# Attention and token mixing on one core: values in column tiles, keys in halves of 32, shared triangles, another order of the engines' work

## The chip, the cores and the metric

The kernel runs on one core of a Trainium2 chip. The metric is device time in microseconds of one launch, from inputs in HBM to the output in HBM. The engines that matter are TensorE (PE), ScalarE (ACT), VectorE (DVE), GpSimd (POOL) and SyncE (SP), which issues the transfers. Each runs its own instructions in the order of its program and waits on semaphores of the others.

## The reference

Sequence 2048, width 512, 32 heads of 16, a causal window of 256 keys, and a token-mixing MLP of 1792, all with two modulated layer norms:

```python
mod = (_silu(c) @ w_mod).reshape(c.shape[0], 6, 1, -1)
h = _layernorm(x) * (1 + ca) + sa
qkv = (h @ wqkv).reshape(B, S, 3, H, Dh).transpose(2, 0, 3, 1, 4)
scores = einsum('bhqd,bhkd->bhqk', q, k) * Dh ** (-0.5)
mask = (i - j >= 0) & (i - j < 256)          # i: query, j: key
p = softmax(where(mask, scores, -1e9))
o = einsum('bhqk,bhkd->bhqd', p, v) -> (B, S, D) @ wo
x = x + ga * o
h = _layernorm(x) * (1 + cb) + sb
h = _layernorm(h)
u = gelu(einsum('bsd,sf->bdf', h, w1) + b1)
y = einsum('bdf,fs->bds', u, w2) + b2        # then transposed back
x = x + gb * y
```

## The kernel before

**Groups and units.** The tokens are taken in four groups G of 512. `proj(G)` normalises the group's tokens (`xn`), transposes them by DMA into `h1T` and projects queries, keys and values. The attention works in units: 256 queries (a half group, `H`) and eight heads (`g8`, one of four). That is 32 units. PE handles a unit in four tiles of 32 rows, two heads of 16 in each, so that four matmuls run side by side, one per tile `j`.

**Keys, values and sums.** `KT` holds, for each block of 64 keys, 128 columns: the 64 keys with the rows of one head of the two (the other's rows zeroed with `mask_par`), then the same with the rows of the other. So the 128 output partitions of a score matmul are two heads times 64 keys, and its columns are queries. `VT` has the same order of rows, with 32 columns for the two heads, and zeros where the head doesn't match. `ones_bd` has it too, and gives the sums of the softmax. The value and sum matmuls are column tiles: four of 32 columns run side by side.

To make `VT`, group 0 projects values with the two parities in two column tiles of 64. From group 1 on, `v` (L972) computes 128 tokens in the natural order, so that half of each tile has to change partitions: `e_vx` swaps it by two DMAs on SP (`vs<-vb`), and `e_vp` places the own and the swapped half with `tensor_copy`, on POOL or DVE. `VT[1]` is zeroed by POOL and `VT[2]` by two DMAs for it.

**Chunks.** The scores of a unit cover eight blocks of 64 keys, of which the first and last per query block are triangles, computed whole and then masked. They are cut into chunks of 512 columns: NEAR, FAR, and half of MID, which two units share (`pair`, L438). A pair of units thus has five chunks. There are 14 pairs; the four units of the first half group have five chunks of their own. That gives 75 chunks, and chunk numbers below count from 0.

For each chunk `attention` (L1161) issues: scores (`S`, into `pss`, three banks, and `psb`, one), two exponentials on ACT (`EA` of 1536 elements and `EB` of 512, into `et`), a masking multiplication on DVE (`M`). When a unit's chunks are through, the values and sums (`AV`, into `po`), then a logarithm and an exponential on ACT (`lz`, the inverse of the sum), and a product on DVE (`OT`).

**Around it.** `post(G)` multiplies with `wo` (`pa`), adds to x, and runs two layer norms (`h`, `hb`) on POOL and DVE. `partials` accumulates the first MLP matmul (`pu`) over the `hb` that exist, between the chunks; `tail` does the rest after the last chunk (`pu`), the gelu, and the last matmul (`py`).

**The order.** All work up to `py` is a list of 1165 operations (`op`). `ORDER` (L62) is a list of their numbers, and `run_schedule` (L164) emits them in it. `CHOSEN` (L118) names the engine for those that have a choice. So each engine's program order is written out by hand. A run of PE work between two `AV` is split into column tiles, too, when it is short (`NEAR_RUN`, `Op.quad`, `mm` at L415), since the array then keeps its shape.

Every instruction is recorded through a helper, so most of the profile has one line number, L256, and groups are told apart by their tiles.

Of the kernel before, what the change touches and what calls it, by code (L numbers as in the profile page):

```python
# [10 lines left out]
ALU = mybir.AluOpType  # L11
# [5 lines left out]
H = 32  # L17
# [6 lines left out]
KB = 64  # L24
HQ = 4 * KB
# [190 lines left out]
def kernel(  # L216
# [31 lines left out]
    class Ordered:  # L248
        def __init__(self, engine):
            self.engine = engine  # L250
# [1184 lines left out]
```

## Time and profile before

| | |
|---|---|
| median of 3 runs | 254.74 us (253.11, 255.09, 254.74) |
| span of the profiled execution | 252.3 us |
| median above that span | 2.4 us |
| granted TensorE clock | 1.000 over the span |
| start of chunk 0's first exponential | 11.2 us |
| start of chunk 70's first exponential | 162.0 us |
| matmuls | 3949 |

The profile is of one execution, and its own time is not listed apart from its span; what lies around the span is taken as the difference to the median. Times inside it count from its start. A busy share says how long an engine had something in flight. For PE that includes the tail of each pipelined matmul, so that short ones side by side look longer than the columns that they stream. ACT and DVE also overlap an instruction's end with the next one's start; the pace is read from starts.

### The profile page before, as it was taken

To read this page: it belongs to the slowest core of one execution; us is meant where nothing else is said; L and a number is where in the kernel's file an instruction comes from. 1 tells how busy PE (TensorE), PEld (TensorE's weight loads), DVE (VectorE), ACT (ScalarE), POOL (GpSimd) and SP (SyncE) were. 2 spreads that over 40 slices of the span, in tenths; PEclk is the share of its full clock that TensorE was granted. 3 is DMA by queue.
4 is the path that set the end of the run, shared out by engine and by line. 5 is a ranking of instruction groups with operands and counts; after the bars stand their busy time and mean duration, and the time that the engine had idled before them with its cause. 6 is when DMAs were issued, how large, how long until landed. Compare 5 with 4: busy or idle time off the path is not lost.

```text
span 252.3 us, 9189 instructions
## 1 busy us (share of the span) xinstructions
PE 235.3 (93%) x3949; PEld 126.0 (50%) x3949; DVE 205.4 (81%) x408; ACT 179.5 (71%) x254; POOL 126.3 (50%) x228
## 2 busy tenths in 40 slices
PE   7988888899987889999999999999999999999995
PEld 2656644445554544555546454556444444444443
DVE  5499998989989998999897999999978764444443
ACT  4699998999999999999999999997147510000000
POOL 8268968795899989845886348173000000000000
PEclk9999999999999999999999999999999999999999
DMA  6999364356055200003401536314999201111111
GB/s 200 323 351 294 48 47 86 44 70 187 3 74 112 53 23 3 4 3 104 131 3 45 155 82 189 105 44 113 343 388 386 108 22 43 44 52 52 42 44 42
DMA packets 42625, 28.13 MB, mean 111 GB/s; under 512 B 12376, under 2 KB 38488, under 8 KB 42584
## 3 DMA queue, kind: packets, MB, share of 16 engines
q1 hardware_dynamic: 42576, 27.54, 39.4%
q8 instruction: 31, 0.51, 0.9%
q14 instruction: 10, 0.08, 0.1%
q10 hardware_dynamic: 8, 0.00, 0.0%
HBM read 22.03 MB, written 2.10 MB: 96 GB/s over the span
## 4 chain that ended last, share of the span: by engine, by line
PE 52%; ACT 24%; DVE 7%; DMA 5%; issue 5%; POOL 4%; SPq 1%; POOLq 0%; DVEq 0%
ACT et L256 20%; PE py L256 19%; PE pu L256 16%; PE po L256 5%; PE pss L256 5%; ACT lz L256 3%; PE pa L256 3%; DMA x<-in_A_x_dram 2%; DVE et L256 2%; DMA h1T<-xn 2%; DMA wmod<-in_w_mod_dram 1%; POOL h1T L256 1%; PE pq L256 1%; DVE st L256 1%; PE pk L256 1%
## 5 line engine op out<-in xcount | busy, mean ns | idle before, releaser
L256 ACT ACTIVATE et<-pss 128x1536 bf16<-128x1536 f32 x75 | 110.7, 1476 | 2.8 <-PE psb L256 2.3
L256 PE MATMUL py<-guT,w2r 128*128 128x512 bf16 (+2 forms) x238 | 48.7, 366 | 0.0
L256 ACT ACTIVATE et<-psb 128x512 bf16<-128x512 f32 x75 | 46.9, 626 | 0.0
L256 DVE TENSOR_TENSOR et<-et,maskt 128x1024 bf16<-128x1024 bf16 (+2 forms) x79 | 46.4, 603 | 0.1
L256 PE MATMUL pu<-hb,w1s 128*32 128x512 bf16 (+1 forms) x302 | 39.0, 380 | 0.2 <-DVE QT L256 0.2
L256 PEld LDWEIGHTS <-w2r 128*128 128x128 bf16 x238 | 22.8, 98 | 26.1 <-issue 0.3
L256 PE MATMUL pss<-QT,KT 32*128 32x64 bf16 (+3 forms) x720 | 29.9, 230 | 6.2 <-ACT et L256 3.5
L256 PE MATMUL po<-et,VT 128*32 128x64 bf16 (+3 forms) x960 | 32.2, 234 | 1.3 <-DVE kb L256 0.6
L256 PE MATMUL po<-et,ones_bd 128*32 128x256 bf16 (+3 forms) x624 | 31.7, 268 | 0.0
L256 PEld LDWEIGHTS <-KT 32*128 32x128 bf16 x960 | 17.1, 92 | 28.5 <-issue 24.6
L256 DVE TENSOR_TENSOR otile<-py,xr 128x512 bf16<-128x512 f32 (+2 forms) x17 | 11.2, 660 | 24.4 <-PE py L256 24.2
L256 POOL TENSOR_SCALAR KT<-kb,mask_par 128x512 bf16<-128x512 bf16 (+1 forms) x36 | 25.0, 707 | 11.4 <-DVE kb L256 11.1
L256 PE MATMUL psb<-QT,KT 32*128 32x64 bf16 (+3 forms) x240 | 29.3, 231 | 0.0
L256 PEld LDWEIGHTS <-VT 128*32 128x32 bf16 x960 | 20.8, 96 | 13.2 <-issue 4.7
L256 PE MATMUL pk<-h1T,wqkv 128*32 128x512 bf16 (+4 forms) x228 | 21.1, 340 | 2.4 <-DVE OT L256 1.0
L256 DVE BATCH_NORM_STATS2 st<-x 128x6 f32<-128x512 bf16 x32 | 21.5, 680 | 2.1 <-DMA x<-in_A_x_dram 2.1
L256 PEld LDWEIGHTS <-wqkv 128*32 128x32 bf16 (+1 forms) x350 | 15.3, 96 | 12.7 <-issue 4.7
L256 PEld LDWEIGHTS <-w1s 128*32 128x32 bf16 (+1 forms) x302 | 14.1, 97 | 15.0 <-issue 1.5
L256 PE MATMUL pv<-wqkv,h1T 128*32 128x512 bf16 (+2 forms) x202 | 17.1, 348 | 1.3 <-DVE OT L256 0.7
L256 PE MATMUL pu<-hb,w1r 128*128 128x512 bf16 (+1 forms) x96 | 17.9, 380 | 0.0
L256 PE MATMUL pa<-wod,OT 128*32 128x512 bf16 (+1 forms) x136 | 17.2, 381 | 0.0
L256 PEld LDWEIGHTS <-ones_bd 128*32 128x32 bf16 x624 | 15.8, 97 | 0.1
(109 smaller groups left out, 350.1 us busy)
## 6 DMA issues: line engine op xcount, KB each, us to landing
w2r<-in_B_w_dram SPq DMA_DIRECT2D x14, 512.0 KB, 10.2
w1s<-in_B_w_dram SPq DMA_DIRECT2D x19, 256.0 KB, 4.0
w1r<-in_B_w_dram SPq DMA_DIRECT2D x9, 256.0 KB, 4.3
x<-in_A_x_dram SPq DMA_DIRECT2D x16, 128.0 KB, 5.2
wmod<-in_w_mod_dram SPq DMA_DIRECT2D x4, 512.0 KB, 7.8
out_dram<-otile SPq DMA_DIRECT2D x15, 128.0 KB, 1.7
wmod<-in_w_mod_dram SPq DMA_DIRECT2D x4, 256.0 KB, 3.9
wqkv<-in_A_wqkv_dram SPq DMA_DIRECT2D x4, 256.0 KB, 5.7
```

The lines of the kernel that those rows point to most:

```text
L256: ins = call(*args, **kwargs)
```

## The change

1. **Keys in halves of 32.** A block's 128 columns in `KT` become (half, parity, 32 keys) where they were (parity, 64 keys). `ones_bd`, `mask_half` and the masks follow. `emit_masks` builds ten masks of 32 columns, with 6 selections and 16 copies on POOL (4 and 6 before).
2. **Values in column tiles.** `values` projects 32 tokens of one parity per matmul, in four column tiles, so that the result stands in the rows where `VT` needs it, in all groups. The swap by DMA, its copies and the zeroing of `VT[1]` and `VT[2]` are gone; `place` multiplies with `mask_half` and writes zeros with the values. `v` counts as `AV` for the rule on short runs.
3. **Shared triangles.** In the first four of the 14 pairs (two of group 0, two of group 1), NEAR and FAR take the parts of the triangles' blocks that are not empty, and the 32 x 32 triangles that remain go into a middle chunk of 256 columns: a lower triangle in the rows of the first half of the keys, an upper one in those of the second. The exponentials of that chunk have 768 and 256 elements. Two masks then write two copies of it, each with the other half's rows zero, and the values take both.
4. **Another order.** `ORDER` and `CHOSEN` are new throughout, and each instruction depends, without a semaphore, on the one before it on its engine.

```diff
-NEAR = [(-1, 0, 4, 0), (0, 0, 4, 256)]
-FAR = [(-2, 0, 3, 0), (3, 3, 1, 192), (-4, 0, 1, 256), (1, 1, 3, 320)]
-MID = [(-3, 0, 2, 0), (2, 2, 2, 128)]
+MIXED = 4
+NEAR = [(-1, 0, 8, 0), (0, 0, 8, 256)]
+FAR = [(-2, 0, 6, 0), (3, 6, 2, 192), (-4, 0, 2, 256), (1, 2, 6, 320)]
+MID = [(-3, 0, 4, 0), (2, 4, 4, 128)]
+NEAR_MIXED = [(-1, 0, 7, 0), (3, 7, 1, 224), (-4, 0, 1, 256), (0, 1, 7, 288)]
+FAR_MIXED = [(-2, 0, 5, 0), (2, 5, 3, 160), (-3, 0, 3, 256), (1, 3, 5, 352)]
...
                 if pinned[0]:
                     tc.keep_in_program_order(ins)
+                    if self.last is not None:
+                        tc.add_manual_dep(ins.ins, self.last, ...)
+                    self.last = ins.ins.name
...
+    def values(dst, h1T, tb, n):
+        wv = wqkv[:, :, 2 * D : 3 * D].rearrange("p j (a two d) -> p j two a d", two=2, d=DH)
+        for dc in range(ND):
+            for r in range(4):
+                tok = tb * P + n * KB + r // 2 * QB
+                te.matmul(
+                    dst[QB * r : QB * (r + 1), n, :].rearrange("p (a d) -> p a d", d=DH),
+                    lhsT=h1T[:, dc, tok : tok + QB], rhs=wv[:, dc, r % 2, :, :],
+                    start=(dc == 0), stop=(dc == ND - 1), tile_position=(0, QB * r), skip_group_check=True,
+                )
+
+    def place(eng, dst, src, tb, half):
+        eng.tensor_scalar(
+            out=dst[:, 2 * tb : 2 * tb + 2, :, half * DH : (half + 1) * DH],
+            in0=src[:].rearrange("p i (a d) -> p i a d", d=DH),
+            scalar1=mask_half[:, half : half + 1], scalar2=0.0, op0=ALU.mult, op1=ALU.add,
+        )
...
-            vx = op("vx", "SP", 1.05, e_vx, deps=[ve_op], pos=pos, extra=0.1)
-            own = op("vo", {"POOL": 0.78, "DVE": 0.45}, 0.78, lambda e: e_vp(e, True), deps=[ve_op] + war + zeros[r3], pos=pos)
-            b = op("vp", {"POOL": 0.78, "DVE": 0.45}, 0.78, lambda e: e_vp(e, False), deps=[vx] + war + zeros[r3], pos=pos)
+            vx = op("vx", "SP", 0.0, lambda e: None, deps=[ve_op], pos=pos, extra=-2.0)
+            placed = [
+                op(("vo", "vp")[half], {"POOL": 0.78, "DVE": 0.45}, 0.78,
+                   lambda e, half=half: place(ENGINE[e], VT[r3], box["vb", tb], tb, half), deps=[ve_op] + war, pos=pos)
+                for half in range(2)
+            ]
...
+                for unit, kb, qs, nq, col in pieces:
+                    if kb is not None:
+                        score(unit, kb, QB * qs, QB * nq, col)
+                    else:
+                        for qb in range(4):
+                            for side in range(2):
+                                score(unit, qb - 4 * side, KB * qb + QB * side, QB, col + QB * qb, side)
...
+                if masks is None:
+                    halves = et_of[i][:].rearrange("p j (h n s) -> p h j n s", h=2, s=KB)
+                    src = halves[:, 0]
+                    for m0, dst in ((UPPER, halves[:, 1]), (LOWER, src)):
+                        msk = m[:, m0 : m0 + KB].unsqueeze(1).unsqueeze(1).to_broadcast([P, 4, 4, KB])
+                        ve.tensor_tensor(out=dst, in0=src, in1=msk, op=ALU.mult)
+                    return
...
+                if kb is None:
+                    for side in range(2):
+                        for qb in range(4):
+                            value(0, qb - 4 * side, KB * qb + QB * side, QB, col + 256 * side + QB * qb)
```

In `score`, a `side` picks one half of the 128 columns of `KT`, so the tile has 32 rows and 64 columns, and the two halves go to the lower and the upper 64 partitions of the same bank.

Laid side by side, the two built programs differ like this in what each engine does (instructions):

| engine | before | after |
|---|---|---|
| PE | 3949 matmuls, the array's shape changes 160 times | 4807 matmuls, 640 of 32 columns; 158 changes |
| ACT | 75 large exponentials | 71 large and 4 of 768 elements; two copies of keys, one of queries and one of values more |
| DVE | 12 + 12 multiplications of h; 2 splits of keys; 4 copies into VT | 7 + 7; 8; 6 placements into VT |
| POOL | 44 copies into VT, 8 placements, 4 + 4 multiplications of h | none, 26, 9 + 9 |
| SP | 24 swaps, 2 zeroings | none |

More of the change, by code (lines that the diff above doesn't have):

```diff
@@ L24 @@
 KB = 64
+QB = 32
 HQ = 4 * KB
@@ L175, in run_schedule @@
     for run in runs:
-        sums = [n for n, o in enumerate(run) if o.name == "AV"]
+        sums = [n for n, o in enumerate(run) if o.name == "AV" or o.name == "v"]
         if run[0].cls == "AV" and sums:
@@ L250, in __init__ @@
             self.engine = engine
+            self.last = None
         def __getattr__(self, name):
@@ L300 @@
     wod = const.tile([P, ND, D], BF, name="wod")
-    maskt = const.tile([P, 3, KB], BF, name="maskt")
+    maskt = const.tile([P, 10, QB], BF, name="maskt")
     ones_bd = const.tile([P, 2 * DH], BF, name="ones_bd")
     nc.gpsimd.memset(ones_bd[:], 0.0)
-    nc.gpsimd.memset(ones_bd[0:KB, 0:DH], ZSCALE)
-    nc.gpsimd.memset(ones_bd[KB:P, DH : 2 * DH], ZSCALE)
+    for r in range(4):
+        nc.gpsimd.memset(ones_bd[QB * r : QB * (r + 1), r % 2 * DH : (r % 2 + 1) * DH], ZSCALE)
     nothing = const.tile([P, D], BF, name="nothing")
@@ L316 @@
     QT = [[kvpool.tile([P, D], BF, name=f"QT{r}_{g}") for g in range(ND)] for r in range(2)]
-    KT = [[kvpool.tile([P, 8, 2, KB], BF, name=f"KT{r}_{g}") for g in range(ND)] for r in range(3)]
+    KT = [[kvpool.tile([P, 8, 2, 2, QB], BF, name=f"KT{r}_{g}") for g in range(ND)] for r in range(3)]
     VT = [kvpool.tile([P, 8, DH, 2 * DH], BF, name=f"VT{r}") for r in range(3)]
@@ L440, in pair @@
             u["parts"] = [len(chunks) + n for n in cs]
-        chunks.append((piece_list(a, NEAR), 0, 512, [(192, 128, 1, 512, 0)]))
-        chunks.append((piece_list(a, FAR), 0, 512, [(128, 128, 2, 128, 0)]))
-        chunks.append((piece_list(a, MID) + piece_list(b, MID, 256), 0, 512, [(64, 128, 2, 256, 0)]))
-        chunks.append((piece_list(b, NEAR), 0, 512, [(192, 128, 1, 512, 0)]))
-        chunks.append((piece_list(b, FAR), 0, 512, [(128, 128, 2, 128, 0)]))
+        box["pairs"] = box.get("pairs", 0) + 1
+        if box["pairs"] <= MIXED:
+            shapes = (NEAR_MIXED, [(192, 64, 2, 64, HALVES)]), (FAR_MIXED, [(128, 64, 2, 192, HALVES)])
+            mid = [(a, None, 0, 0, 0), (b, None, 0, 0, 128)], 0, 256, None
+        else:
+            shapes = (NEAR, [(192, 128, 1, 512, BOTH)]), (FAR, [(128, 128, 2, 128, BOTH)])
+            mid = piece_list(a, MID) + piece_list(b, MID, 256), 0, 512, [(64, 128, 2, 256, BOTH)]
+        for unit in (a, b):
+            for pieces, masks in shapes:
+                chunks.append((piece_list(unit, pieces), 0, 512, masks))
+            if unit is a:
+                chunks.append(mid)
     for G in range(NG):
@@ L627 @@
         0: [],
-        1: [op("z", "POOL", 3.45, lambda e: po.memset(VT[1][:], 0.0), ready=2.0, pos=-22.0)],
+        1: [op("z", "POOL", 0.05, lambda e: None, pos=-22.0)],
     }
@@ L812, in e_v @@
                     box["v", tb] = bank([P, 2, 256], F32, "pv")
-                wv = wqkv[:, :, 2 * D : 3 * D].rearrange("p j (a two d) -> p j two a d", two=2, d=DH)
-                tok = slice(tb * P + n * KB, tb * P + (n + 1) * KB)
-                for dc in range(ND):
-                    for par in range(2):
-                        te.matmul(
-                            box["v", tb][KB * par : KB * (par + 1), n, :].rearrange("p (a d) -> p a d", d=DH),
-                            lhsT=h1T[:, dc, tok], rhs=wv[:, dc, par, :, :],
-                            start=(dc == 0), stop=(dc == ND - 1), tile_position=(0, KB * par),
-                        )
+                values(box["v", tb], h1T, tb, n)
             def e_ve(e):
@@ L974, in e_v @@
                 if n == 0:
-                    box["v", tb] = bank([P, D], F32, "pv")
-                for dc in (2 * n, 2 * n + 1):
-                    mm(
-                        box["v", tb][:], h1T[:, dc, tb * P : (tb + 1) * P], wqkv[:, dc, 2 * D : 3 * D],
-                        (dc == 0), (dc == ND - 1),
-                    )
-            def e_ve(e):
-                vb = box["vb", tb] = work.tile([P, 2, 256], BF, name="vb", tag=vb_tag, bufs=1)
-                copy(
-                    e, vb[:].rearrange("p two (a d) -> p a two d", d=DH),
-                    box["v", tb][:].rearrange("p (a two d) -> p a two d", two=2, d=DH),
-                )
-            def e_vx(e):
-                vs = box["vs", tb] = work.tile([P, 256], BF, name="vs", tag=vs_tag, bufs=1)
-                dma.dma_start(out=vs[0:KB, :], in_=box["vb", tb][KB:P, 0, :])
-                dma.dma_start(out=vs[KB:P, :], in_=box["vb", tb][0:KB, 1, :])
-            def e_vp(e, own):
-                for half in range(2):
-                    rows = slice(KB * half, KB * half + KB)
-                    block, src = (half, box["vb", tb][rows, half, :]) if own else (1 - half, box["vs", tb][rows, :])
-                    ENGINE[e].tensor_copy(
-                        out=VT[r3][rows, 2 * tb + block, :, half * DH : (half + 1) * DH],
-                        in_=src.rearrange("p (a d) -> p a d", d=DH),
-                    )
-            vb_tag, vs_tag = turn("vb"), turn("vs")
+                    box["v", tb] = bank([P, 2, 256], F32, "pv")
+                values(box["v", tb], h1T, tb, n)
+            def e_ve(e):
+                box["vb", tb] = work.tile([P, 2, 256], BF, name="vb", tag=vb_tag, bufs=1)
+                copy(e, box["vb", tb][:], box["v", tb][:])
+            vb_tag = turn("vb", 3)
             war = [av_ops[G - 2, g] for g in range(ND)] if G >= 2 else []
@@ L1153, in partials @@
                 ]
-    masks_built = op("masks", "POOL", 2.6, lambda e: emit_masks(), deps=zeros[1], pos=-20.0)
+    masks_built = op("masks", "POOL", 4.75, lambda e: emit_masks(), deps=zeros[1], pos=-20.0, ready=2.55)
     ea_ops, eb_ops = [], []
```

130 lines of the change are left out of this document (73 added, 57 removed), and 123 rows, old and new, of tables (CHOSEN, ORDER).

## The prediction

> **What bounds the kernel now.** I read the page from the top: busy shares, slices, then the costliest groups, then windows cut, to 0.2 us, at the start of every fifth chunk of the attention, then the chain of waits.
>
> ```profile
> span 252.3 us, 9189 instructions
> PE 235.3 (93%) x3949; PEld 126.0 (50%) x3949; DVE 205.4 (81%) x408; ACT 179.5 (71%) x254; POOL 126.3 (50%) x228
> PE   7988888899987889999999999999999999999995
> ACT  4699998999999999999999999997147510000000
> ```
>
> ScalarE (ACT) is full until slice 28 (about 175 us) and then nearly done; TensorE (PE) looks full everywhere, yet its busy time counts the pipeline's tail behind every short matmul. So the first 175 us have two candidates, and the last 75 us one.
>
> ```profile
> 22.20:33.10 10.90, 9.16 (x264) 6.42 (x262) 10.72 (x27) 10.89 (x17) 10.52 (x16) 1.00 0.52 109
> 33.10:44.40 11.30, 9.93 (x237) 5.30 (x235) 10.50 (x21) 10.63 (x15) 7.76 (x15) 1.00 0.53 59
> 44.40:54.90 10.50, 9.60 (x244) 5.39 (x243) 9.66 (x23) 10.50 (x16) 9.12 (x19) 1.00 0.46 53
> 54.90:65.50 10.60, 9.96 (x251) 5.48 (x248) 10.15 (x20) 10.59 (x16) 6.97 (x13) 1.00 0.45 127
> 65.50:76.00 10.50, 9.00 (x230) 5.12 (x230) 9.63 (x19) 10.42 (x14) 10.01 (x15) 1.00 0.33 46
> 76.00:87.50 11.50, 9.50 (x250) 5.33 (x243) 11.47 (x22) 10.79 (x15) 10.58 (x15) 1.00 0.40 90
> 161.90:178.50 16.60, 16.60 (x357) 9.51 (x354) 16.38 (x37) 13.49 (x24) 6.86 (x11) 1.00 0.32 87
> 178.50:252.30 73.80, 70.98 (x342) 32.75 (x340) 42.94 (x81) 12.23 (x20) 0.00 (x0) 1.00 0.35 128
> ```
>
> The columns are length, then busy time of PE, weight loads, DVE, ACT, POOL. The first six windows are the first six pairs of units, five chunks each. ACT is busy 10.42 to 10.89 of every 10.5 to 11.5 us; in the sixth it is DVE that is full (11.47 of 11.50). The last window holds only dense matmuls.
>
> ```profile
> L256 ACT ACTIVATE et<-pss 128x1536 bf16<-128x1536 f32 x75 | 110.7, 1476 | 2.8 <-PE psb L256 2.3
> L256 ACT ACTIVATE et<-psb 128x512 bf16<-128x512 f32 x75 | 46.9, 626 | 0.0
> 44.57 1.45 ACT L256 ACTIVATE et<-pss 128x1536 bf16<-128x1536 f32 x1
> 45.90 0.61 ACT L256 ACTIVATE et<-psb 128x512 bf16<-128x512 f32 x1
> 46.38 0.41 ACT L256 ACTIVATE lz<-po 128x256 f32<-128x256 f32 x1
> 46.64 1.48 ACT L256 ACTIVATE et<-pss 128x1536 bf16<-128x1536 f32 x1
> ```
>
> Starts, not durations, give ACT's pace: the large exponential holds it 1.33 us (44.57 to 45.90), the small one 0.48, a logarithm of 256 elements 0.26; the exponential that inverts it, of as many, I take at 0.3. A pair of units needs 5 x 1.81 + 2 x 0.56 = 10.2 us of ACT, against 10.5 to 11.5 measured. ACT sets the pace of the attention, and half a microsecond per pair is lost beside it.
>
> ```profile
> 31.75 4.04 DMA h1T<-xn
> ...
> 178.50 22.45 PE pu L256 x104
> 200.94 2.81 PE py L256 x13
> 203.78 45.75 PE py L256 x225
> ```
>
> The first row is one of the chain's stops on a transfer, in the second pair. The others, its end, are 74 us of matmuls without a gap. The change leaves their number and shape alone; by the built programs PE has 77.8 us of matmul work behind the last scores after it, 78.2 before. So only an earlier end of the attention can shorten the kernel.
>
> **The sum, part by part.** *Shared triangles, on ACT.* In the first four pairs the middle chunk shrinks from 1536 and 512 elements to 768 and 256. The two rates differ by 1024 elements and 0.85 us, 0.83 ns an element, so a chunk saves 0.64 + 0.21 = 0.85 us, four save 3.4. It lies on the path, since ACT sets the pace there.
>
> *Evacuations that move to ACT.* In the built program ACT does two more copies of keys, one more of queries and one more of values, and one fewer scaling of h1T.
>
> ```profile
> L256 ACT ACTIVATE kb<-pk 128x256 bf16<-128x256 f32 x1 | 0.4, 366 | 0.0
> L256 ACT ACTIVATE part<-pu 128x512 f32<-128x512 f32 x1 | 0.6, 600 | 0.0
> L256 ACT ACTIVATE h1T<-h1T,modFM 128x256 bf16<-128x256 bf16 x2 | 1.1, 593 | 0.3 <-DVE modFM L256 0.3
> ```
>
> One copy has 256 columns, three have 512: 0.37 + 3 x 0.60 - 0.59 = 1.6 by durations, 1.2 if each overlaps its neighbour by 0.1. ACT nets -2.2 us.
>
> *Shared triangles, on PE.* The columns streamed stay the same within 0.4 us, but 858 more matmuls carry them (4807 against the page's 3949), 640 of only 32 columns. What one costs is in no row; the nearest are these.
>
> ```profile
> 73.44 0.21 PE L256 MATMUL pss<-QT,KT 32*128 32x64 bf16 x3
> 73.47 0.21 PE L256 MATMUL pss<-QT,KT 32*128 32x64 bf16 x3
> 73.50 0.26 PE L256 MATMUL pss<-QT,KT 32*128 32x192 bf16 x3
> 6.71 0.54 PE L256 MATMUL ps_fm<-sT,wmod 128*128 128x1 bf16 x16
> ```
>
> Four matmuls of 64 columns in four row tiles start 0.03 us apart as a set, at most 7.5 ns each; sixteen one-column matmuls of the full array take 0.54 us, 34 ns each. The lower end is columns alone: nothing, or -0.4. At 7.5 ns, a shared chunk's 64 score matmuls take 0.48 us where 512 columns took 0.21 (+0.27), the 32 value matmuls of a unit 0.24 where 256 columns took 0.11 (+0.13), and the extra corner pieces of the near chunks 0.07 a unit: 4 x 0.27 + 8 x 0.13 + 8 x 0.07 = 2.7 us. At 34 ns it is 640 x 0.031 = 20 us. I take 7.5 ns, the row being of the same tiled kind. Does it reach the path? Counting columns at 0.217 us per 512 (45.75 us is 225 matmuls, some short) and 0.1 us for each of ten changes of array shape per pair, PE then holds 10.2, 9.3, 9.2 and 8.7 us in the four pairs, ACT 9.35 plus the moved copies. They just fit side by side: zero on the path, 2.7 if the cover is gone.
>
> The Trainium skill (the page "TensorE: Matmul & The Clock Gate", section "Wait — 56ns, not 53.3ns?") has a floor of about 25 ns from start to start, however few the columns. This trace disagrees for tiled matmuls, by the 7.5 ns just read, and is near it for the full array. By that figure the 640 would cost an estimated 14 us.
>
> *Values in tiles.* Twelve token tiles stream the same 2048 columns, now as 32 matmuls in four column tiles: nothing on PE. The swap through DMA goes, with its copies.
>
> ```profile
> L256 POOL COPY VT<-vs 64x256 bf16<-64x256 bf16 x24 | 10.8, 452 | 3.9 <-DMA vs<-vb 3.0
> L256 POOL COPY VT<-vb 64x256 bf16<-64x256 bf16 x20 | 10.2, 511 | 3.5 <-DVE vb L256 2.9
> L256 POOL TENSOR_SCALAR VT<-vb,mask_half 128x512 bf16<-128x512 bf16 x8 | 5.8, 731 | 1.3 <-DVE vb L256 1.3
> L256 POOL MEMSET VT<- 128x4096 bf16 x1 | 3.5, 3517 | 0.1
> L256 POOL TENSOR_TENSOR h<-h,bc_cb 128x512 bf16<-128x512 bf16 x4 | 5.3, 1328 | 4.1 <-DVE h L256 4.0
> L256 POOL TENSOR_TENSOR h<-h,bc_sb 128x512 bf16<-128x512 bf16 x4 | 4.7, 1177 | 0.3
> ```
>
> POOL loses 10.8 + 10.2 + 3.5 = 24.5 us and gains 18 x 0.73 = 13.2 for placing values, about 2 for the longer masks, and five tiles' two multiplications, 5 x 2.5 = 12.5; smaller moves cancel. The sum is level. What is new is that values no longer wait for a landing (3.0 us on POOL, none of it directly before a matmul), and 26 transfers leave SP's queue, in which the transposes of the next group stand.
>
> *DVE and the order.* DVE loses those ten multiplications and four copies and gains eight splits of keys and six placements of values; the masks are level (four more of 1024, eight halved). At the 0.45 us below for a multiplication, 0.4 to 0.7 for a copy and an estimated 0.4 for a split or a placement its total falls by about 2 us, and the new order evens it out.
>
> ```profile
> L256 DVE TENSOR_TENSOR et<-et,maskt 128x1024 bf16<-128x1024 bf16 x43 | 31.8, 742 | 0.1
> L256 DVE TENSOR_TENSOR h<-h,bc_cb 128x512 bf16<-128x512 bf16 x12 | 5.4, 448 | 0.9 <-POOL h L256 0.8
> L256 DVE CAST QT<-pq 128x512 bf16<-128x512 f32 x12 | 8.2, 683 | 1.6 <-PE pq L256 1.5
> PE pk L256 <- DVE OT L256: 1.0, 1, 1.0
> PE pv L256 <- DVE OT L256: 0.7, 1, 0.7
> ```
>
> The last two rows are waits between 70 and 92 us: PE stood for a PSUM bank that DVE was to empty. Counted in the program between the masks of chunks 30 and 35, DVE held 12.6 us of work; now 9.4, and the fullest stretch (chunks 20 to 25) 11.5. The sixth window should fall from 11.5 to the 10.5 of its neighbours: -1.0.
>
> Elsewhere I expect the same half microsecond per pair. In the last pairs PE's work moves about (chunks 55 to 65 lose 1.9 us, 65 to 75 gain 1.1), which I cost at zero because ACT has the same 10.2 per pair; if ACT is not late there, 1.1.
>
> Sum: -2.2 on ACT, 0 on PE, -1.0 on DVE: the span goes from 252.3 to 249.1. The median of three runs is 254.74, 2.4 above the profiled span; I keep that 2.4 outside. Forecast 251.5 us.
>
> **Rivals.** *More than the sum.* Waits that I left alone vanish as well: the chain stands 4.04 us for a transpose of h1T at 31.75, and the window 33.1 to 44.4 is 0.8 longer than the next. If two such windows fall to 10.5 and the evacuations hide, the span loses 2 to 4 more: 247.5 to 249.5. The shorter queue speaks for it; that nothing in it brings x or the weights sooner speaks against it. Chance 0.15.
>
> *The gain is swallowed.* PE takes over as the late engine in the four pairs (10.2 in the first already matches 9.35 plus copies and waits), so 2.7 us of small matmuls eat the 3.2: 254 to 256. For it, PE's busy 9.2 to 10 in each of these windows; against it, that this counts tails. Chance 0.15.
>
> *Slower: the 32-column matmuls are issued slowly.* Their score tiles are 32 rows by 64 columns, a shape that the trace does not have. At p ns each the extra is 640 x (p - 3.3) ns. The four pairs offer about 4 x 0.7 us of room on PE, and 3.2 us are gained, so it turns at 6 us, p = 13 ns. At 16 to 20 ns it costs 8 to 11 us, less that 6: 257 to 260; at 34 ns 268. Against it stands the 7.5 ns. The floor that the Trainium skill's page gives would mean this rival, at an estimated 14 - 6 = 8 us more. Chance 0.12.
>
> *The new order does not hold.* Its queues are in order, and one late POOL result (two multiplications of h are 2.5 us there, 0.9 on DVE) holds hb and so the partial sums of PE; each such stop is about 1 us, as the two waits above. Five of them give 256 to 259. Chance 0.13.
>
> **How the numbers follow.** The forecast has 0.45, from 249.5 to 253.5: no time shows the 1.2 of moved copies and the 1.0 on DVE exactly, which makes that width. I count 1%, 2.5 us, as the least that a measurement tells from no change. Faster by more than that means under 252.2: two thirds of the forecast and all of the first rival, 0.30 + 0.15 = 0.45. Slower means over 257.3: the slow issue with 0.12 and two thirds of the order's case, 0.09: 0.21. The rest, 0.34, lies within. A range from 247.5 to 257.5 leaves out the slow issue, most of the order's tail and little below, about 0.2.
>
> **What would show it.** Right: the large exponential in two sizes, 71 at 1.48 us and 4 near 0.8; the four windows of the mixed pairs at about 10.0 us each; no vs tile; the last pair's first exponential near 158.7 us instead of 161.9; the dense end still 74 us. Wrong: score sets of 32 columns that start more than 0.05 us apart per four, or idle ACT in front of exponentials in the mixed pairs with PE as the releaser (swallowed, or slow issue); PE waiting for hb or for a bank that DVE or POOL empties (order); a dense end with gaps, which no part of the sum foresees.

## The result: 3.5% slower

The changed kernel takes 262.73 us (median of 4 runs, 261.71 to 263.19) against 254.09 us (4 runs, 253.11 to 255.09): a ratio of 1.035, 95% interval 1.030 to 1.040. The forecast was 251.5 us, and the time lies above its range of 247.5 to 257.5. In the later sets of runs the kernel before had medians of 253.55 to 253.68 us. One run each of e5 and e6 below was slow, at a lower granted clock than the fastest (0.987 and 0.988), and is left out of their medians.

The page of the changed kernel:

```profile
span 260.8 us, 10838 instructions
...
PE 238.6 (92%) x4807; PEld 134.4 (52%) x4807; DVE 209.9 (81%) x406; ACT 178.4 (68%) x257; POOL 128.5 (49%) x222
...
PE   7988979868898589998999999999999999999995
...
ACT  4698988969899599999899999999325630000000
...
q8 instruction: 37, 0.61, 1.0%
```

The span grew by 8.5 us. ACT's row, nearly all nines before, now has holes in its first half, the deepest in slices 9 and 14 (52 to 59 and 85 to 91 us). DVE's busy time, which was to fall by 2 us, rose by 4.5. The end is unchanged, as its chain shows (start, length, work):

```profile
187.28 22.45 PE pu L259 x104
209.72 48.40 PE py L259 x238
```

The dense matmuls begin at 187.28 us in place of 178.50 and then need 73.5 us, 0.3 less than before. All of the loss lies in the attention. Windows cut at every fifth chunk show where (length, then busy time of PE, weight loads, DVE, ACT, POOL):

```profile
23.00:35.00 12.00, 10.56 (x332) 6.69 (x321) 10.65 (x22) 10.46 (x17) 11.18 (x17) 1.00 0.43 88
35.00:47.70 12.70, 10.55 (x440) 7.45 (x443) 11.20 (x23) 11.09 (x19) 7.64 (x14) 1.00 0.22 15
47.70:60.80 13.10, 10.30 (x389) 6.31 (x374) 10.08 (x23) 10.31 (x16) 11.03 (x18) 1.00 0.33 44
81.90:95.90 14.00, 9.51 (x290) 6.51 (x286) 13.97 (x21) 11.03 (x16) 13.65 (x13) 1.00 0.11 13
```

The first three are pairs 1 to 3: 12.0, 12.7 and 13.1 us where 10.9, 11.3 and 10.5 stood, and ACT no longer fills them. The last is pair 6: 14.0 us in place of 11.5, with DVE full (13.97) and POOL nearly so. (The expectations below count the stretch ahead of the pairs as the first stage, so that their seventh stage is pair 6.) These four windows hold 7.6 us of the loss; pair 9 adds 1.1.

The list of waits names two kinds that are new:

```profile
ACT et L259 <- PE psb L259: 7.5, 10, 1.8
...
PE pss L259 <- issue: 2.3, 3, 1.3
...
PE pv L259 <- DVE vb L259: 2.2, 1, 2.2
...
PE po L259 <- issue: 1.8, 3, 0.8
...
PE po L259 <- DVE vb L259: 1.6, 1, 1.6
```

ACT waits 7.5 us for scores (2.3 before). PE in turn waits for values that DVE copies, and, under "issue", for nothing that the profile names. PE's timeline shows where:

```profile
48.88 0.30 PE L259 MATMUL po<-et,VT 128*32 128x96 bf16 x8 [0.67 <-issue]
...
51.84 0.20 PE L259 MATMUL pss<-QT,KT 32*64 32x32 bf16 x3
...
51.96 0.18 PE L259 MATMUL psb<-QT,KT 32*64 32x32 bf16 x1
...
53.43 0.20 PE L259 MATMUL pss<-QT,KT 32*64 32x32 bf16 x3 [1.29 <-issue]
...
57.16 0.25 PE L259 MATMUL po<-et,VT 128*32 128x160 bf16 x4 [0.83 <-issue]
```

Between 51.84 and 51.96 stand 32 of the 32-column score matmuls, about 4 ns each: they are not slow. Yet PE stops for 1.29 us in the middle of a set, at 53.43. Counting PE's instructions, each matmul with its weight load, in the built program beside these records gives the pattern: eight gaps over 0.2 us between 24 and 66 us, 6.5 us in all, end at one and the same place of every 256 instructions. (A gap is the time from one matmul's start to the next one's, less 0.42 ns for each column of the first; 512 columns take 0.216 us from start to start.) The kernel before has none there that the profile leaves without a releaser. The page's q8 row fits: 37 transfers of 16 KB on the instruction queue, and 9614 instructions are 37.6 times 256; before, 31 transfers and 7898 instructions, 30.9 times 256. The trace also has the time of each of these transfers, and that settles it. Each of the eight gaps ends 1.3 to 1.9 us after a transfer has ended: the longest, at 53.43, 1.6 us after the transfer from 50.92 to 51.82. And the next transfer starts 1.0 to 2.0 us after PE has gone on. In the kernel before, PE comes to this place 2.0 us or more after the transfer. So PE's program arrives in blocks, and here PE reaches the end of one before the next is there.

The second kind shows in DVE's groups and timeline and in POOL's timeline:

```profile
L259 DVE TENSOR_TENSOR et<-et,maskt 128x1024 bf16<-128x1024 bf16 x39 | 32.4, 836 | 0.3
...
L259 DVE TENSOR_TENSOR h<-h,bc_sb 128x512 bf16<-128x512 bf16 x7 | 5.0, 716 | 0.2
L259 DVE TENSOR_TENSOR h<-h,bc_cb 128x512 bf16<-128x512 bf16 x7 | 4.2, 605 | 0.0
```

```profile
82.15 2.80 DVE L259 TENSOR_TENSOR et<-et,maskt 128x512 bf16<-128x512 bf16 x2
84.86 0.68 DVE L259 CAST vb<-pv 128x512 bf16<-128x512 f32 x1
...
85.80 1.38 DVE L259 TENSOR_TENSOR h<-h,bc_cb 128x512 bf16<-128x512 bf16 x1
87.21 1.26 DVE L259 TENSOR_TENSOR h<-h,bc_sb 128x512 bf16<-128x512 bf16 x1
```

```profile
81.94 1.17 POOL L259 TENSOR_TENSOR h<-h,bc_cb 128x512 bf16<-128x512 bf16 x1
83.18 1.21 POOL L259 TENSOR_TENSOR h<-h,bc_sb 128x512 bf16<-128x512 bf16 x1
...
85.67 1.22 POOL L259 TENSOR_TENSOR h<-h,bc_cb 128x512 bf16<-128x512 bf16 x1
86.97 1.22 POOL L259 TENSOR_TENSOR h<-h,bc_sb 128x512 bf16<-128x512 bf16 x1
```

Two masks that take 0.41 us each elsewhere need 2.80 us together, a multiplication 1.38, while POOL runs its own two-input multiplications. The copy of the values to `vb` stands behind them, and PE behind that copy. The group means rose from 742, 500 and 448 ns.

So two theories stood at the start: **F**, PE's instructions arrive too slowly where matmuls are dense; and **C**, two-input work on POOL stretches DVE. Their rivals were **W**, the shared triangles cost PE's own time; **O**, the new sequence is bad by itself; and **A**, evacuations moved to ACT lengthen stages that ACT paces.

### The profile page after: what moved, and what is told of

It reads as the page before. It is cut to its first block, busy times and chain, and to the rows that moved or that the text cites. A ratio compares the mean times of both kernels' runs of the same rounds, so it can differ in the third digit from the quotient of the medians.

```text
span 260.8 us, 10838 instructions
## 1 busy us (share of the span) xinstructions
PE 238.6 (92%) x4807; PEld 134.4 (52%) x4807; DVE 209.9 (81%) x406; ACT 178.4 (68%) x257; POOL 128.5 (49%) x222
## 4 chain that ended last, share of the span: by engine, by line
PE 54%; ACT 17%; DVE 11%; issue 7%; DMA 6%; POOL 4%; SPq 1%; DVEq 0%; POOLq 0%
PE py L259 19%; PE pu L259 16%; ACT et L259 15%; PE po L259 6%; PE pss L259 6%; PE pk L259 3%; DVE et L259 3%; PE pa L259 2%; DMA x<-in_A_x_dram 2%; DVE st L259 2%; DMA h1T<-xn 2%; ACT lz L259 2%; DVE h L259 2%; PE pv L259 2%; DMA wmod<-in_w_mod_dram 1%
## 5 line engine op out<-in xcount | busy, mean ns | idle before, releaser
L259 ACT ACTIVATE et<-pss 128x1536 bf16<-128x1536 f32 (+1 forms) x75 | 107.5, 1434 | 9.9 <-PE psb L259 7.5
L259 DVE TENSOR_TENSOR et<-et,maskt 128x512 bf16<-128x512 bf16 (+2 forms) x83 | 52.0, 645 | 0.7 <-ACT et L259 0.4
L259 ACT ACTIVATE et<-psb 128x512 bf16<-128x512 f32 (+1 forms) x75 | 45.2, 604 | 0.0
L259 PE MATMUL po<-et,VT 128*32 128x32 bf16 (+7 forms) x1216 | 33.7, 219 | 5.5 <-issue 1.8
L259 PE MATMUL pss<-QT,KT 32*64 32x32 bf16 (+8 forms) x912 | 31.4, 218 | 6.6 <-ACT et L259 2.6
L259 PEld LDWEIGHTS <-KT 32*128 32x128 bf16 (+1 forms) x1216 | 18.4, 94 | 28.7 <-issue 25.7
L259 PE MATMUL psb<-QT,KT 32*64 32x32 bf16 (+8 forms) x304 | 30.9, 219 | 0.0
L259 POOL TENSOR_SCALAR KT<-kb,mask_par 128x512 bf16<-128x512 bf16 (+1 forms) x30 | 20.8, 707 | 12.7 <-DVE kb L259 12.5
L259 POOL TENSOR_SCALAR VT<-vb,mask_half 128x512 bf16<-128x512 bf16 x26 | 20.1, 782 | 5.3 <-DVE vb L259 5.3
L259 PE MATMUL pv<-wqkv,h1T 128*32 128x256 bf16 x512 | 17.7, 274 | 3.7 <-DVE vb L259 2.2
L259 PEld LDWEIGHTS <-wqkv 128*32 128x32 bf16 (+1 forms) x404 | 14.9, 96 | 10.9 <-issue 4.2
```

What stands on the lines that cost most here:

```text
L259: ins = call(*args, **kwargs)
```

## The experiments

| run | order | shared triangles | other edit | us | ratio to before, 95% |
|---|---|---|---|---|---|
| changed kernel | new | pairs 1-4 | | 262.73 | 1.030-1.040 |
| e1 | new | none | | 258.15 | 1.014-1.021 |
| e2 | old | pairs 1-4 | | 259.72 | 1.017-1.026 |
| e3 | old | none | | 253.63 | 0.997-1.002 |
| e4 | before | | sums in 128 columns | 254.11 | 1.000-1.005 |
| e5 | new | pairs 1-4 | engines of h as before | 267.38 | 1.044-1.057 |
| e6 | before | | sums in 64 columns | 277.95 | 1.090-1.101 |
| e7 | old | pairs 1-4 | projections not cut | 259.19 | 1.019-1.024 |
| e8 | old | none | projections not cut | 255.75 | 1.005-1.018 |
| e9 | old | pairs 1, 3, 5, 7 | | 258.66 | 1.016-1.025 |
| e10 | old | none | 5 evacuations on ACT | 254.53 | 1.002-1.006 |
| e11 | new | pairs 1-4 | POOL: one-input | 258.39 | 1.016-1.021 |
| e12 | new | pairs 1-4 | POOL: one-input, twice | 259.61 | 1.018-1.027 |
| e13 | old | pairs 1, 3, 5, 7 | POOL: one-input | 257.75 | 1.015-1.020 |
| e14 | old | none | POOL: one-input | 252.70 | 0.994-1.000 |
| e15 | new | none | POOL: one-input | 254.56 | 1.003-1.007 |
| e16 | new | pairs 1, 3, 5, 7 | POOL: one-input | 256.65 | 1.008-1.017 |

All but e4 and e6 have the values in column tiles and the keys in halves of 32. Every number under "us" is a median.

### Which part of the change costs: e1, e2, e3

```
-MIXED = 4
+MIXED = 0            # e1, e3
-ORDER, CHOSEN of the change
+ORDER, CHOSEN of before   # e2, e3
```

> The changed kernel with MIXED = 0: the four pairs are plain again (4295 matmuls for 4807), all else and the new order stay. Theory F (PE runs out of fetched instructions where small matmuls stand close; in the changed kernel eight of its idle gaps, 6.5 us, lie at the same place of every 256 instructions): at most two such gaps are left, under 1.5 us, ACT gets its 3.4 us back, and the time is 256 to 258.5 us. Theory O (the new order is at fault, by DVE and POOL work that PE waits for): little goes, and the plain pairs cost ACT's 3.4 us: 261 to 265 us.

> The changed kernel with the ORDER and CHOSEN of before: values in column tiles and shared triangles stay (4813 matmuls). Theory F: gaps at the block places stay, 4 us or more in the four pairs, and the time is 257 to 262 us. Theory O: the loss goes with the order, and the 3.4 us of ACT show: 250 to 253 us.

> The ORDER and CHOSEN of before and MIXED = 0: of the change only halves of 32 and values in column tiles remain (4301 matmuls). Theory F: few or no gaps at the block places, 253 to 256.5 us. Theory O: as before or better by the waits for the swap, 252 to 254.5 us. It tells the two apart only together with the run that has shared triangles in this order.

Values in tiles and keys in halves alone change nothing (253.63). The shared triangles add 6.1 us in the old order and 4.6 in the new; the new order adds 4.5 without them and 3.0 with them. So neither is the whole cause. The three times lie in theory F's ranges, and e1 has one block gap left (0.9 us). In pairs 1 to 4, e3 and e2 compare like this:

```profile
22.20:64.70 42.50, 37.84 (x1101) 24.31 (x1098) 40.50 (x85) 42.49 (x60) 35.35 (x55) 1.00 0.36 64
```

```profile
22.70:70.70 48.00, 40.98 (x1541) 27.30 (x1538) 42.21 (x89) 40.55 (x59) 33.87 (x57) 1.00 0.30 56
```

ACT is full in the first (42.49 of 42.50); in the second its busy time is 1.9 us lower and it stands idle for 7.5. PE's busy time grew by 3.1 us for 440 matmuls, 7 ns each, and its idle time by 2.4: together the 5.5 us by which this stretch is longer. The 1541 matmuls with their weight loads are 12.0 blocks of 256, one in 4.0 us; the 1101 are 8.6, one in 4.9. In e2 six gaps over 0.2 us fall at the same place of a block, 2.9 us together, four of them in these pairs, with 2.4 us. Theory F had expected 4 us or more there, so in the old order it accounts for less than half of the loss; PE's own time (W) fits the rest. e3 has one gap of 0.2.

### Instructions alone: e4, e6

```
-                value(1, 0, q, width, col)
+                for d in range(0, width, 128):      # e4; 64 in e6
+                    value(1, 0, q + d, min(128, width - d), col + d)
```

> The kernel before with each sum matmul of 256 columns cut into pieces of 128: 592 more matmuls, the same columns, order and results. Theory F: gaps at one place of every 256 instructions appear where the attention is densest, 1 to 4 us in all, 255 to 258 us. If only columns and the start-to-start of tiled matmuls count (under 7.5 ns each in the trace), nothing changes: 253.5 to 255 us.

> The kernel before with each sum matmul of the attention cut into pieces of 64 columns: 5725 matmuls in place of 3949, the same columns in all, nothing else changed. Theory F (PE's instructions arrive in blocks of 256, and a block takes at least about 3.7 us): PE shows waits without a releaser that lie at one and the same place of every 256 of its instructions, in the stretches where a block is used up in under 3.7 us, and the time rises to 258 to 266 us. Rival W (every further matmul costs some 4 to 7 ns of PE's own time and nothing else): 1776 of them are 7 to 12 us of PE time, of which the room of the early pairs hides most; no such periodic waits, 254 to 258 us.

Both cut the sum matmuls of the kernel before, the same columns in more pieces. Cut in two, 592 matmuls more, they cost 0.6 us (+0.3%), with no gap over 0.44 us at a block boundary: theory F's 255 to 258 was missed. Cut further, 1776 more, they cost 24.3 us, above what theory F had said and far above W's 254 to 258. The page of e6, then its waits and its timeline on PE:

```profile
q8 instruction: 44, 0.72, 1.2%
```

```profile
PE po L256 <- issue: 15.1, 12, 3.6
```

```profile
92.88 0.40 PE L256 MATMUL po<-et,VT 128*32 128x192 bf16 x14 [1.33 <-issue]
...
114.59 0.24 PE L256 MATMUL po<-et,ones_bd 128*32 128x64 bf16 x7 [1.25 <-issue]
...
132.47 0.21 PE L256 MATMUL po<-et,ones_bd 128*32 128x64 bf16 x3 [1.58 <-issue]
...
196.70 0.38 PE L256 MATMUL po<-et,ones_bd 128*32 128x64 bf16 x27 [3.60 <-issue]
```

PE's waits without a releaser before `po` alone are 15.1 us. Put beside the program, eighteen gaps of 0.3 to 3.8 us, 22.4 us in all, end at one place in a block of 256, each 1.2 to 1.7 us after a transfer on the instruction queue has ended. The span of this execution is 22.2 us longer than that of the kernel before (274.5 against 252.3), so the gaps are as long as the whole loss; PE's busy time rose by 4.5 us besides, and other waits shrank. Nothing of the change is in this kernel, so theory F holds by itself: instructions that come too densely stop PE at block boundaries.

### Less dense: e7, e8

```
-NEAR_RUN = 7
+NEAR_RUN = 0
```

No projection is cut into four column tiles any more: 474 fewer matmuls and 58 more changes of shape.

> Shared triangles in four pairs with the order of before, as in the second run, but with no projection cut into four 32-column tiles: 4339 matmuls in place of 4813, the same work and more changes of tile shape (217 in place of 159). Theory F: fewer instructions in the same stretch, so the stalls at block boundaries shrink: 256 to 258.5 us where 259.7 was measured, and the step from the run beside it without shared triangles is 3 to 4.5 us in place of 6.1. Rival W (the shared triangles' own PE time is the whole cost): the changes of shape come on top, 260 to 263 us, and the step stays 5.5 to 6.5.

> The same without shared triangles: 3827 matmuls, order of before, values in column tiles, no projection cut into four. Control for the run beside it. Both theories: the changes of shape cost some 58 times 0.05 to 0.1 us of PE time, part of it beside ACT: 253.5 to 257 us where 253.6 was measured with the cuts.

The step from e8 to e7 is 3.4 us, within what F had said (3 to 4.5) and below W's 5.5 to 6.5, but the four runs of e8 spread over 2.9 us, so that this alone is weak; the gaps at block boundaries fell from 2.9 to 1.7 us. But the uncut projections cost 2.1 us themselves, so e7 is hardly faster than e2 (259.19, expected 256 to 258.5), and it is no way out.

### POOL and DVE: e5, e11, e12

> The changed kernel with one thing taken back: for the 28 operations that make h (normalising, the two-input multiplication, the two-input addition) the engine is chosen as before, so that fewer two-input multiplications run on POOL; order, shared triangles and everything else stay. Theory C (two-input work on POOL stretches the DVE instructions beside it): the mean of the 1024-element masks falls from 836 ns back to near 742, the waits of PE for vb (2.2 and 1.6 us) go, the seventh stage falls from 14.0 to 11 to 12 us, and the time from 262.7 to 259 to 261 us; the stalls at the start (pairs 1 to 3) stay. Rival O (the order alone is bad, whichever engine multiplies): the seventh stage stays above 13 us and the time at 262 to 263.5.

```
-    "POOL": [..., 246, 250, 252, 477, 707, 713, ...]
+    "DVE": [..., 246, 250, 252, 477, 707, 713, ...]
```

(The diff shows the multiplications; normalisations and additions followed the choices of before.) This went wrong: 267.38 us. The masks' mean fell, to 789 ns, but pair 6 stayed at 13.5 us and pair 5 rose to 12.5. DVE has the work itself now, in an order that was laid out without it; that this is the reason was not tested. So moving work off POOL and taking away the contention are two things; the next runs keep the engines and change only how many inputs POOL reads.

```
+                if e == "POOL":
+                    for _ in range(2):      # 4 in e12
+                        po.tensor_scalar(out=u[:], in0=u[:], scalar1=1.0, scalar2=0.0, op0=ALU.mult, op1=ALU.add)
+                    return
                 ENGINE[e].tensor_tensor(out=u[:], in0=u[:], in1=bc_cb1[:], op=ALU.mult)
```

> The changed kernel in which POOL, for the nine tiles of h that it scales and shifts, runs two one-input operations (times 1.0, plus 0.0) in place of the two two-input ones: it leaves the scale and the shift of these tiles out of the computation. Theory C (two-input work on POOL stretches DVE instructions beside it, and DVE paces the seventh stage): masks of 1024 elements fall from a mean of 836 ns to 740 to 760, the two h operations of DVE that took 1.38 and 1.26 us fall to about 0.42, the seventh stage falls from 14.0 to 11.3 to 12.5 us and the time from 262.7 to 259.5 to 261 us. Rival O (the order puts more work into this stage than the engines can do, stretched or not): masks as quick as that, but the stage stays at 13 us or more and the time at 262 to 263.5.

> The same with four one-input operations in place of the two two-input ones, so that POOL is not relieved (about 3 us for a tile where the two took 2.4): scale and shift of these tiles are left out. Theory C: DVE as quick as in the run beside it; the seventh stage 11.5 to 13 us and the time 260 to 262, since POOL itself is now later. Rival P (what helps in the run beside it is POOL's own time, not DVE's): stage and time as in the changed kernel or worse, 262.5 to 266.

e11 takes 258.39 us, 4.3 less than the changed kernel; e12, in which POOL is not relieved, 259.61, 3.1 less. Pair 6 of e11, then of e12, as windows:

```profile
80.60:92.40 11.80, 9.49 (x290) 6.51 (x286) 11.77 (x21) 10.86 (x16) 11.36 (x14) 1.00 0.08 15
```

```profile
79.20:91.50 12.30, 9.51 (x290) 6.53 (x286) 12.27 (x21) 10.87 (x16) 11.67 (x15) 1.00 0.02 4
```

The same 21 instructions of DVE hold it 11.77 and 12.27 us in place of 13.97. The same rows as above, in e11's timeline of DVE:

```profile
80.85 1.70 DVE L259 TENSOR_TENSOR et<-et,maskt 128x512 bf16<-128x512 bf16 x2
...
83.41 0.83 DVE L259 TENSOR_TENSOR h<-h,bc_cb 128x512 bf16<-128x512 bf16 x1
84.27 0.71 DVE L259 TENSOR_TENSOR h<-h,bc_sb 128x512 bf16<-128x512 bf16 x1
```

2.80 became 1.70, 1.38 and 1.26 became 0.83 and 0.71. Theory C holds for DVE's times in this stage, and rival O, which had it at 13 us or more, is out. The sizes were missed. The masks' mean fell to 788 ns where 740 to 760 was expected (746 in e12), and the times fell further than 259.5 and 260.

One reason is that "two-input" was too narrow: one-input operations of POOL stretch DVE too. In e11 the 20 masks of 1024 elements with such an operation beside them took a median of 0.86 us, the 19 others 0.68. The Trainium skill ("GPSIMD Engine Reference", section "Specifications") says that GpSimd shares its SBUF interfaces with VectorE, with contention for DVE instructions in a 2-port perf mode or with two SBUF inputs; masks and multiplications are of the second kind, and the runs agree, with the sizes just given.

What the contention is worth is better read by stages than from the medians. Against the changed kernel, e11 is 3.7 us shorter in pairs 6 to 10, and 1.1 in pairs 1 to 3. The latter can't be POOL's doing, since its first multiplication of the changed kernel starts at 81.9 us. e12 is only 1.7 us shorter in pairs 6 to 10, and 2.8 in pairs 1 to 3, where the same program had gaps of 3.1 us at block boundaries in place of 6.5. So up to 2.0 of the 3.7 us may be POOL's own time (rival P), and of the 3.1 us between the medians of e12 and the changed kernel a part is the gaps, which differ from one execution to the next.

### Evacuations on ACT: e10

```
-    "DVE": [..., 95, 100, 108, 280, 284, ...]
+    "ACT": [..., 95, 100, 108, 280, 284, ...]
```

> The third run (order of before, no shared triangles, 253.6 us) with one thing of the change alone: the five evacuations of projections that the new order gives to ACT in the first six stages (kb, vb and QT) go from DVE to ACT. Theory A (without the shared triangles ACT paces these stages, so that each moved evacuation lengthens them): ACT's busy time there rises by some 2.3 us and the time to 255.3 to 256.3 us, which would be about half of the 4.5 us that the new order costs without shared triangles. Rival O (the sequence itself costs all of it, and DVE gains as much as ACT loses): 253 to 254.3 us.

254.53 us, 0.9 above e3, between the two expectations. In the first four stages of e1, then of e3, the windows add up to:

```profile
sum 46.10, PE 39.83 PEld 26.71 DVE 40.95 ACT 44.78 POOL 37.09; mean PE 9.96 PEld 6.68 DVE 10.24 ACT 11.19 POOL 9.27
```

```profile
sum 42.70, PE 37.87 PEld 25.71 DVE 40.38 ACT 42.61 POOL 35.60; mean PE 9.47 PEld 6.43 DVE 10.10 ACT 10.65 POOL 8.90
```

ACT's busy time is 2.2 us longer with the new order. In e10, which moves the evacuations alone, it is 1.5 us longer than in e3 in these stages, and they take 1.4 us more; 0.9 is left between the medians.

### Shared triangles spread out: e9, e13 to e16

```
-MIXED = 4
+MIXED = (1, 3, 5, 7)
...
-        if box["pairs"] <= MIXED:
+        if box["pairs"] in MIXED:
```

> Order of before, values in column tiles, shared triangles again in four of the 14 pairs, but in pairs 1, 3, 5 and 7 in place of 1 to 4: the same 4813 matmuls as in the second run, never two shared pairs behind one another. Theory F with the shared triangles' own PE time (about 0.8 us in a pair, against 0.85 us saved on ACT): the blocks of 256 are used up more evenly, so of the 6.1 us that the four pairs in a row cost most goes, but PE has no time left to give: 253.5 to 256.5 us. Rival F alone (PE's own time for the shared triangles lies beside ACT): with the stalls gone the saving on ACT appears, 250 to 252.5 us. Rival W (only the number of matmuls counts): as in a row, 258.5 to 260.5 us.

A miss: of the gaps at block boundaries one is left (0.6 us, the others of e2 are gone), as F had said, and still 258.66 us came out, only 1.1 less than e2. The time is also above the 253.5 to 256.5 expected. The next four separate this from POOL's multiplications (e13 to e16 leave the scale and the shift of POOL's tiles out, like e11).

> The ninth run (order of before, shared triangles in pairs 1, 3, 5 and 7) with one-input operations in place of POOL's two-input ones, as in the eleventh: the scale and the shift of the tiles that POOL makes are left out. With neither stalls nor stretched masks: if the 5.0 us that the ninth run still cost were the masks that fell beside POOL's multiplications (theory C), then it comes within 1 us of the run beside it without shared triangles, or below it; if it is PE's own time for the shared triangles (theory W), it stays 2 to 4 us above it.

> Control: order of before, no shared triangles, one-input operations on POOL in place of the two-input ones (scale and shift of these tiles left out). Theory C: the order of before has eight two-input operations on POOL and three masks beside them, which it stretches by about 0.2 to 0.4 us each; 252.0 to 253.7 us where 253.6 was measured.

> The first run (new order, no shared triangles, 258.15 us) with one-input operations on POOL (scale and shift of its nine tiles left out). Theories A and C together: without the stretched DVE instructions some 3 us of the order's 4.5 go, and the evacuations on ACT leave about 1: 254.5 to 256 us. The eleventh run less this one is then what the shared triangles alone cost in the new order: theory F says 3 to 5 us.

> The eleventh run (changed kernel, one-input operations on POOL, 258.4 us) with the shared triangles in pairs 1, 3, 5 and 7 in place of 1 to 4. Theory F: the waits at one place of every 256 instructions, 6.0 us there, fall under 3 us, and the time to 255 to 257; theory W (PE's own time): 257.5 to 259 us.

Spread triangles cost 5.1 us in the old order without two-input work on POOL (257.75 against 252.70), as much as with it, so theory C does not explain e9; theory W's 2 to 4 us was missed too. Under the new order, which was made for shared triangles, they cost 2.1 us spread (256.65 against 254.56) and 3.8 in a row (258.39), and the gaps at block boundaries go from 6.6 us (e11) to 2.9 (e16): F's expectation for e16 held. In e13 the three pairs that follow a shared one (2, 4 and 6) lose 3.5 us against e14, the shared pairs themselves 1.3. Almost half of the loss sits in pair 6, which has no shared triangles itself, but follows pair 5, which has. Pair 6 in e13, then in e14:

```profile
77.50:90.80 13.30, 9.84 (x355) 6.63 (x359) 13.00 (x24) 11.05 (x16) 9.93 (x11) 1.00 0.30 72
```

```profile
75.40:86.40 11.00, 9.31 (x273) 6.14 (x277) 10.97 (x20) 10.83 (x15) 9.40 (x10) 1.00 0.37 86
```

DVE is full in both. Ahead of it stand the masks of pair 5's middle chunk, in DVE's timeline of e13 and of e14:

```profile
75.89 2.10 DVE L262 TENSOR_TENSOR et<-et,maskt 128x1024 bf16<-128x1024 bf16 x2
```

```profile
73.83 0.92 DVE L262 TENSOR_TENSOR et<-et,maskt 128x1024 bf16<-128x1024 bf16 x1
```

A shared chunk has its masks in two pieces of 1024 elements at one place, where an unshared one has a single piece and leaves the rest to the far chunks. The sum of the masks is the same; where they stand in DVE's queue is not, and in this stage DVE has no room. PE also stops once at a block boundary in pair 6 of e13, as its timeline shows:

```profile
90.07 0.29 PE L262 MATMUL po<-et,ones_bd 128*32 128x256 bf16 x4 [0.63 <-issue]
```

This is a reading of one stage. How the 5.1 us divide between the masks, the gaps, PE's own time and the other stages was not separated.

## Why the prediction was wrong

Taken one after another, the medians step up like this: 252.70 (e14), +1.9 for the new order (e15), +3.8 for the shared triangles in a row (e11), +4.3 for two-input work on POOL under the new order: 262.7. By stages, 3.7 of the last step lie where POOL multiplies. The kernel before has about 0.9 of it too (e3 less e14).

**What bounds the kernel** was read rightly: ACT paced the attention, and the dense end kept its 74 us.

**Shared triangles on ACT** and the **moved evacuations** were of the right size as work. The large exponential now comes in two sizes:

```profile
L259 ACT ACTIVATE et<-pss 128x1536 bf16<-128x1536 f32 x71 | 104.3, 1469 | 7.2 <-PE psb L259 4.9 <-PE pss L259 1.8
...
L259 ACT ACTIVATE et<-pss 128x768 bf16<-128x768 f32 x4 | 3.2, 811 | 2.7 <-PE psb L259 2.6
```

That is 0.66 us less for a large one, and 0.24 for a small one (617 ns to 380): 0.90 a chunk where 0.85 was forecast. But ACT's busy time in the four pairs fell by only 1.9 us, not 3.4 (e2 against e3). The idle time behind the bar, ahead of the exponentials, was the forecast's "wrong" sign. The evacuations, priced at 1.2 us, measured 0.9 in e10.

**Shared triangles on PE: this step failed**, not in its price but in where it lies. 2.7 us of small matmuls were forecast, and PE's busy time rose by 3.1 (e2 against e3). But the prediction wrote "They just fit side by side: zero on the path". ACT's share of a pair fell, PE's rose, and PE, not ACT, then came last in these pairs: the forecast's second rival. And the count of 858 was priced per matmul only. As 858 times two instructions it is 6.7 more blocks, and from the first to the fourth pair PE ran out of them: 6.5 us of gaps. The rival that issue is slow named the right engine and the right stretch, with the wrong mechanism: the matmuls start about 4 ns apart, faster than the 7.5 assumed, and stop between blocks. The prediction also misread the floor of about 25 ns from start to start that it cites from the Trainium skill ("TensorE: Matmul & The Clock Gate", section "Wait — 56ns, not 53.3ns?"): it called the trace in disagreement for tiled matmuls. Laid beside the tiles of the built program, no two matmuls on one tile start less than 25 ns apart, in either kernel; the 4 and the 7.5 ns are from one tile to the next. The floor holds tile by tile, and with four or eight tiles side by side it does not bring the 14 us estimated from it.

**Values in tiles** was right: nothing gained, nothing lost (e3).

**DVE and the order: this step failed.** POOL's multiplications of five more tiles were counted as POOL's time and found level; DVE's total was to fall by 2 us and the sixth window to 10.5. What the multiplications do to DVE beside them had no term. DVE rose by 4.5 us, the window to 14.0. With one-input operations in their place DVE's total is 204.7 us (e11), 0.7 below the kernel before, and pairs 6 to 10 are 3.7 us shorter; up to 2.0 of these may be POOL's own time. The rival "the new order does not hold" had its sign and its waits, PE behind a copy of DVE; but POOL's result was not merely late, it slowed DVE. What remains of the order without two-input work on POOL, 1.9 us, is half accounted for by the evacuations; the other half stays open.

**Outside the sum**, the earlier queue for transfers (the first rival) shows nowhere as a gain.

No run here beats both kernels by more than can be told. e14 is 0.9 us lower (ratio 0.994 to 1.000) but leaves work out; it suggests how little a POOL without two-input operations could give the kernel before.

## What to carry to other kernels

Cutting matmuls smaller costs instructions, and these have a price of their own: compare the number of PE instructions in the densest stretch, in blocks of 256 with the weight loads counted, with the time that the stretch has, before pricing the matmuls one by one. A move that relieves the pacing engine is worth only the distance to the next one; here the relief of ACT never showed in the time. And an operation moved to POOL is not free when POOL has time: look at which DVE instructions will run beside it.

## What the runs showed of the hardware

- PE's instructions come in transfers of 16 KB on the instruction queue, 31, 37 and 44 of them for 30.9, 37.6 and 44.7 times 256 instructions (the kernel before, the changed kernel, e6). Where a block was used up in about 4 us or less, PE could stand for 0.2 to 3.8 us at the boundary; it went on 1.2 to 1.9 us after the next transfer had ended, and the transfer after that started about 1 to 2 us later. The Trainium skill ("Runtime: NRT & Kernel Launch", section "Instruction fetch mechanics") has the blocks of 256 and calls the crossing mostly hidden. That held in the kernel before (no such gap) and nearly in e4 (4541 matmuls, none over 0.44 us); in e6 (5725) the gaps took 22.4 us.
- A two-input operation on POOL stretched DVE's two-input instructions beside it: in the changed kernel a mask of 1024 elements took a median of 1.21 us with such an operation beside it (7 of them) and 0.68 without (32), a multiplication or addition of h 1.26 (5) against 0.42 (9). Of the 32, the 14 with a one-input operation of POOL beside them took a median of 0.86.
- Score matmuls of 32 columns in tiles of 32 rows by 64 columns ran about 4 ns apart, 32 of them in 0.12 us. They go to eight tiles; on one tile, the next started 31 ns later or more in the changed kernel.
